# Loads of units 6 to 15 moved from GpSimd's queue to SyncE's in a fused attention and feed-forward kernel

## The chip, the cores and the metric

The kernel runs on one core of a Trainium2 chip. The metric is the device time of one execution in microseconds (us). A core has a matrix engine (TensorE, PE in the profile), three engines for elementwise work (VectorE or DVE, ScalarE or ACT, GpSimd or POOL) and SyncE (SP), which here only issues DMA transfers. Each engine works through its own instructions in order; semaphores tie the engines together. A DMA transfer can be issued by GpSimd (the profile's "software_dynamic" queue) or by SyncE ("hardware_dynamic").

## The reference

Linear attention on 8 batches and 8 heads of 576 tokens with 64 dimensions, then a feed-forward layer with an ELU.

```python
q_s = exp(q - max(q, -1)); q_s = q_s / (sum(q_s, -1) + 1e-09)
k_s = exp(k - max(k, 2));  k_s = k_s / (sum(k_s, 2) + 1e-09)     # over the tokens
kv  = einsum('bhsd,bhse->bhde', k_s, v)
x   = einsum('bhsd,bhde->bhse', q_s, kv)      # then (B, S, H*D) -> 4608 x 512
h   = x @ w_in                                # 512 -> 2048
g   = where(h > 0, h, exp(min(h, 0)) - 1)
out = g @ w_out                               # 2048 -> 512, float32
```

## The kernel before

The attention is cut into 16 units (NU): unit n is one half of the heads of batch n // 2. The feed-forward part is cut into nine blocks j of 512 tokens (NBLK).

For each unit, `load` (L321) fetches q, k and v, 576 KB each, into the tiles QR, KR and VR. QR and KR exist twice and are used by odd and even units in turn; VR is one tile for all units from 4 on. `stage1` (L359) takes the exponentials of q and k on ScalarE (L365, L368), casts v to bfloat16 into VB on GpSimd (L373), and on VectorE sums q, takes the reciprocal and scales q into QS (L381, L385, L389). From unit 6 on (BYDMA) the scaled q is transposed by a DMA that SyncE issues (`turn`, L428, QS to QT), and GpSimd widens the result into qsT (`widen`, L435). TensorE forms kv of the unit (`kv_mm`, L461); VectorE divides it into MBLK (`m`, L470, L474); TensorE multiplies it with qsT (`ao_mm`, L491) in two parts, and ScalarE copies the result into XT (`xt`, L513). The second part of unit n and the kv of unit n + 1 are one group of TensorE instructions, which signals once, at its end.

For each block, `hg` (L534) computes the hidden layer in eight groups of 256 features: matmuls on TensorE (L545), exp on ScalarE (L554, into one of two ESB tiles), then in most groups on VectorE a tensor_scalar with min and add (L571) and a maximum with the hidden values in PSUM (L573), which gives GT. A few early groups have another form (L565 on ScalarE, L567 on VectorE). `out_mm` (L577) multiplies GT with w_out (L583), `out_store` (L590) copies the result to one of three OSB tiles (L600) and has SyncE store it in two halves (L609).

The order of instructions on each engine is not that of the code. `Sched` collects all operations with an engine, an estimated duration and dependencies. A dependency is a buffer's reader or writer: a load into KR waits for the kv matmuls that read KR before, a load into QR for the scaling L389, a load into VR for the cast L373. `one_pass` (L132) simulates the engines and at each step takes the operation that can start first, and among nearly equal ones that with the lower key; `fluid` (L107) estimates when transfers land, with one queue for each issuing engine. The result is a fixed list for each engine, and `emit` (L194) writes it out with the semaphore waits ahead of each instruction. A waiting instruction therefore holds back all that follows it on its engine. An operation added under a gate (L727) can't be planned before a certain hidden group has started.

`load` takes the engine as an argument, with GpSimd as default. The loads of units 0 and 1 name SyncE; all others are on GpSimd, together with the loads of the weights, the casts L373 and the widening L435. SyncE has the transposes and the output stores. The call that the diff touches is the helper `loads` in `program` (L698), which hands out the loads of units 4 to 15; those of units 2 and 3 are written out at L655 to L659.

Of the kernel before, what the change touches and what calls it, by code (L numbers as in the profile page):

```python
# [255 lines left out]
class Gen:  # L256
# [357 lines left out]
    def program(self):  # L614
# [50 lines left out]
        def due(n):  # L665

            return when[n][1] + 4 if n in when else 3 + 4 * (n % 2)
# [30 lines left out]
        def loads(*tn):  # L698
            def go():
                for t, n in tn:  # L700
                    if n < NU:
                        self.load(n, t, due(n) - 20)
            return 0, go

        steps = [[first(2)], [wide(2), kv(2), loads(("q", 4), ("k", 4))],
# [110 lines left out]
```

## Time and profile before

| | |
|---|---|
| time, median of 3 runs (lowest to highest) | 311.72 us (311.62 to 311.88) |
| span of the profiled execution | 308.2 us |
| granted TensorE clock | 0.994 |
| TensorE, VectorE, ScalarE, GpSimd busy | 295.3, 202.9, 161.9, 71.5 us |
| GpSimd's issues of q, k and v loads (L329) | 42, about 0.72 us each |
| SyncE's issues: transposes, output stores | 10, 72 |
| DMA traffic | 49.39 MB, mean 160 GB/s |

The span is the time from the first to the last instruction in one profiled execution; it is a little shorter than the time of an unprofiled run. "Busy" counts the time in which an engine executes, and not the time in which it waits, branches or issues a hardware-queue DMA. GpSimd's issue of a DMA does count. GpSimd's waits in this execution were these, from the list of who waited for whom: 65.6 us in 12 waits of a KR load for the kv matmuls, 25.3 us of a VB cast for its v load, 25.2 us of a qsT cast for TensorE, 17.4 us of a QR load for VectorE's L389.

### The profile page before, as it was taken

To read this page: it belongs to the slowest core of one execution; us is meant where nothing else is said; L and a number is where in the kernel's file an instruction comes from. 1 tells how busy PE (TensorE), PEld (TensorE's weight loads), DVE (VectorE), ACT (ScalarE), POOL (GpSimd) and SP (SyncE) were. 2 spreads that over 40 slices of the span, in tenths; PEclk is the share of its full clock that TensorE was granted. 3 is DMA by queue.
4 is the path that set the end of the run, shared out by engine and by line. 5 is a ranking of instruction groups with operands and counts; after the bars stand their busy time and mean duration, and the time that the engine had idled before them with its cause. 6 is when DMAs were issued, how large, how long until landed. Compare 5 with 4: busy or idle time off the path is not lost.

```text
span 308.2 us, 4597 instructions
## 1 busy us (share of the span) xinstructions
PE 295.3 (96%) x1938; PEld 241.3 (78%) x1938; DVE 202.9 (66%) x244; ACT 161.9 (53%) x190; POOL 71.5 (23%) x84
## 2 busy tenths in 40 slices
PE   6889999989999979999999999999999999999994
PEld 6777778768788768888888888888888888888783
DVE  3837946798988969595959596866544445555500
ACT  4658667989657346464646463734343443333311
POOL 0790263441440436050505040301000000000000
PEclk9799999999999999999999999999999999999999
DMA  7999999797488684747383934031111221111122
GB/s 267 328 359 390 389 389 379 263 281 161 152 249 222 187 227 101 239 88 249 87 250 82 246 87 90 20 80 28 34 36 40 46 48 41 34 34 34 36 68 68
DMA packets 29589, 49.39 MB, mean 160 GB/s; under 512 B 13952, under 2 KB 13952, under 8 KB 29568
## 3 DMA queue, kind: packets, MB, share of 16 engines
q0 software_dynamic: 10336, 33.16, 35.2%
q1 hardware_dynamic: 19232, 15.93, 20.1%
q8 instruction: 15, 0.25, 0.3%
q14 instruction: 6, 0.05, 0.1%
HBM read 36.70 MB, written 9.44 MB: 150 GB/s over the span
## 4 chain that ended last, share of the span: by engine, by line
PE 87%; DVE 8%; ACT 3%; DMA 1%; issue 1%
PE PS L583 41%; PE PS L545 40%; PE PS L491 2%; PE PS L461 2%; DVE ESB L571 2%; DVE QS L389 1%; DMA QR<-in_q_dram 1%; DVE GT L573 1%; ACT ESB L554 1%; DVE ZQ L381 1%; DVE GT L567 1%; DVE MBLK L474 1%; PE PS L412 1%; ACT ESB L565 1%; PE PS L648 1%
## 5 line engine op out<-in xcount | busy, mean ns | idle before, releaser
L583 PE MATMUL PS<-W,GT 128*128 128x512 f32 x576 | 144.9, 393 | 1.6 <-DVE GT L573 1.6
L545 PE MATMUL PS<-XT,W 128*128 128x512 f32 x576 | 142.6, 392 | 2.2 <-DVE GT L573 0.8
L545 PEld LDWEIGHTS PS<-XT,W 128*128 128x128 f32 x576 | 107.3, 188 | 26.2 <-DVE GT L567 1.8
L583 PEld LDWEIGHTS PS<-W,GT 128*128 128x128 f32 x576 | 106.2, 188 | 24.1 <-DVE GT L573 2.6
L554 ACT ACTIVATE ESB<-PS 128x1024 f32<-128x1024 f32 x72 | 73.9, 1027 | 93.5 <-PE PS L545 93.3
L571 DVE TENSOR_SCALAR ESB<-ESB 128x1024 f32<-128x1024 f32 x64 | 55.2, 862 | 65.5 <-ACT ESB L554 65.2
L573 DVE TENSOR_TENSOR GT<-ESB,PS 128x1024 fp32r<-128x1024 f32 x64 | 78.1, 1221 | 2.2
L600 ACT ACTIVATE OSB<-PS 128x512 f32<-128x512 f32 x32 | 19.2, 599 | 37.0 <-PE PS L583 37.0
L381 DVE TENSOR_REDUCE ZQ<-QR 128x18 f32<-128x1152 f32 x16 | 21.6, 1349 | 6.5 <-ACT QR L365 6.2
L373 POOL CAST VB<-VR 128x1152 bf16<-128x1152 f32 x15 | 19.9, 1328 | 25.3 <-DMA VR<-in_v_dram 25.3
L329 POOL DMA_DIRECT2D KR<-in_k_dram x14 | 10.2, 726 | 65.6 <-PE PS L461 65.6
L389 DVE TENSOR_TENSOR QS<-QR,RZQ 128x1152 f16<-128x1152 f32 x16 | 21.7, 1358 | 0.6
L513 ACT ACTIVATE XT<-PS 128x640 fp32r<-128x640 f32 (+5 forms) x32 | 19.7, 619 | 3.1 <-PE PS L491 3.0
L365 ACT ACTIVATE QR<-QR 128x1152 f32<-128x1152 f32 x16 | 18.7, 1166 | 3.7 <-DMA QR<-in_q_dram 3.7
L435 POOL CAST qsT<-QT 128x1152 fp32r<-128x1152 f16 x10 | 13.7, 1370 | 29.6 <-PE PS L461 25.2
L368 ACT ACTIVATE KR<-KR 128x1152 bf16<-128x1152 f32 x16 | 18.6, 1162 | 0.8 <-DMA KR<-in_k_dram 0.8
L491 PE MATMUL PS<-qsT,MBLK 128*128 128x320 f32 (+3 forms) x64 | 14.2, 305 | 1.0 <-ACT XT L513 0.6
L491 PEld LDWEIGHTS PS<-qsT,MBLK 128*128 128x128 f32 x64 | 11.6, 189 | 4.4 <-ACT XT L513 1.0
L329 POOL DMA_DIRECT2D QR<-in_q_dram x14 | 10.3, 735 | 17.4 <-DVE QS L389 17.4
L567 DVE SCALAR_TENSOR_TENSOR GT<-PS,ESB 128x1024 fp32r<-128x1024 f32 x8 | 9.8, 1223 | 5.9 <-ACT ESB L565 5.9
L329 POOL DMA_DIRECT2D VR<-in_v_dram x14 | 10.0, 718 | 3.3 <-POOL VB L373 3.3
L648 PE MATMUL PS<-ID 128*128 128x128 f16 x92 | 8.7, 273 | 1.5 <-POOL ID L309 1.5
(28 smaller groups left out, 78.2 us busy)
## 6 DMA issues: line engine op xcount, KB each, us to landing
out_dram<-OSB SPq DMA_DIRECT2D x64, 128.0 KB, 2.4
QR<-in_q_dram POOLq DMA_DIRECT2D x14, 576.0 KB, 5.7
KR<-in_k_dram POOLq DMA_DIRECT2D x14, 576.0 KB, 5.0
VR<-in_v_dram POOLq DMA_DIRECT2D x14, 576.0 KB, 6.0
W<-in_moe_w_in_dram POOLq DMA_DIRECT2D x8, 512.0 KB, 8.1
W<-in_moe_w_out_dram POOLq DMA_DIRECT2D x4, 1024.0 KB, 17.7
QR<-in_q_dram SPq DMA_DIRECT2D x2, 576.0 KB, 4.5
KR<-in_k_dram SPq DMA_DIRECT2D x2, 576.0 KB, 6.9
```

The lines of the kernel that those rows point to most:

```text
L329: S.add(eng, ISSUE[eng], lambda e: e.dma_start(dst, src), key, W=[name], dma=f"{name}{eng}", nbytes=128 * 4608, follow=self.gpq if chain e ...
L373: S.add(eng, t, lambda e: e.tensor_copy(VB[:, hs, :, 0:D], v[:, hs, :, :]), key - 50, R=[vname], W=[f"VB{i}"])
L381: S.add("dve", t_dve(1152) + 60, lambda e: e.tensor_reduce(self.ZQ[i][:, :, :].rearrange("p h c -> p (h c)"), q[:, :, :, :].rearrange("p h ...
L389: S.add("dve", t_dve(1152) + 60, lambda e: e.tensor_tensor(qso, q[:, :, :, :], rz, ALU.mult), key - 3, R=[f"qR{i}", f"RZQ{i}"], W=[f"QS{se ...
L491: last = e.matmul(P[:, f * 512:f * 512 + n_], M[:, f, :], T[:, c0:c1, f * 64:f * 64 + 64], start=True, stop=True)
L513: S.add("act", t_act((h1 - h0) * n_, True), lambda e, dst=dst, src=src: e.activation(dst, src, AF.Copy), key, W=W, X=X)
L545: last = e.matmul(P[:, t * 512:(t + 1) * 512], self.W1[:, kc, tt * 128:(tt + 1) * 128], self.XT[:, kc, rc:rc + BLK], start=(kc == 0), stop ...
L554: S.add("act", t_act(1024, True), lambda e: e.activation(esb[:, :], P[:, :], AF.Exp), key, W=[f"E{i}"], X=banks)
L571: S.add("dve", t_dve(1024, 2) + 80, lambda e: e.tensor_scalar(esb[:, :], esb[:, :], 1.0, -1.0, ALU.min, ALU.add), key, X=[f"E{i}"])
L573: S.add("dve", t_dve(1024) + 90, lambda e: e.tensor_tensor(gt, esb[:, :], P[:, :], ALU.max), key, R=[f"E{i}"], W=gw, X=banks)
L583: last = e.matmul(dst, GT[:, jj, ts * 128:(ts + 1) * 128], self.W2[:, jj, :], start=(jj == 0), stop=(jj == 15))
L600: S.add("act", t_act(512, True), lambda e: e.activation(osb[:, :], src, AF.Copy), key, W=[f"O{i}0", f"O{i}1"], X=[f"b{bk}"])
```

## The change

The helper that issues the loads of units 4 to 15 passes an engine: GpSimd for units 4 and 5, as before, and SyncE from unit 6 on. The 30 loads of units 6 to 15 go from GpSimd's in-order list, and from its software queue, to SyncE's list and its hardware queue, in among the transposes and the output stores. It is meant to free GpSimd, whose casts stand in the same list behind loads that wait for their buffers.

```diff
@@ -699,7 +699,7 @@
             def go():
                 for t, n in tn:
                     if n < NU:
-                        self.load(n, t, due(n) - 20)
+                        self.load(n, t, due(n) - 20, "gp" if n < 6 else "sp")
             return 0, go
```

The planner, which sees other engines and other landing times, also writes a slightly different order for the rest. GpSimd's list shrinks from 77 to 45 rows (a row is a run of equal instructions): between the casts nothing is left from unit 6 on. SyncE's list has, for a typical unit, transpose, q load, two pairs of stores, v load, k load. ScalarE's list puts the exponentials of unit 8 (L365, L368) ahead of the first XT copy of unit 6; TensorE's list puts a hidden group (L545) ahead of each of the two ao parts of unit 6; VectorE's puts the reciprocal L385 of unit 8 earlier and the division L470, L474 of unit 7 one hidden group later. Up to the loads of unit 6 nothing is moved.

## The prediction, made before the changed kernel ran

> **What bounds the kernel now.** I read the page's first two parts, then the chain of waits, then the windows by stage, and then the timelines of TensorE, VectorE and GpSimd in the one stretch where TensorE stands still after the start.
>
> ```profile
> PE 295.3 (96%) x1938; PEld 241.3 (78%) x1938; DVE 202.9 (66%) x244; ACT 161.9 (53%) x190; POOL 71.5 (23%) x84
> ...
> PE   6889999989999979999999999999999999999994
> ...
> PE 87%; DVE 8%; ACT 3%; DMA 1%; issue 1%
> ```
>
> TensorE is busy 295.3 of 308.2 us and carries 87% of the chain, so a change to who issues loads can win back only idle TensorE time, 12.9 us in all. The windows say where that is:
>
> ```profile
> 0.00:40.00 40.00, 34.95 (x295) 29.08 (x295) 25.51 (x37) 25.65 (x29) 17.53 (x27) 0.96 1.10 349
> ...
> 54.00:66.00 12.00, 10.20 (x119) 7.44 (x118) 9.77 (x14) 10.58 (x12) 5.83 (x7) 1.00 0.81 250
> ...
> 100.00:110.00 10.00, 8.36 (x70) 6.66 (x67) 9.37 (x11) 3.92 (x5) 5.53 (x6) 1.00 0.68 179
> ...
> 150.00:200.00 50.00, 50.00 (x326) 41.14 (x324) 38.94 (x45) 26.60 (x32) 14.98 (x14) 1.00 0.51 133
> ...
> 289.00:308.20 19.20, 15.23 (x67) 11.99 (x65) 1.92 (x2) 3.42 (x5) 0.00 (x0) 1.00 0.30 68
> ```
>
> The second number of a row is TensorE's busy time. 5.05 us are lost before 40 us and 3.97 in the tail, which the change doesn't touch (its first moved load is at 54 us, its last before 190). From 110 to 289 us nothing is lost. In between, 1.80 us go in 54 to 66, 0.30 in 72 to 80 and 1.64 in 100 to 110. The last one is a single gap before the L583 at 109.49. Three timelines explain it (start, duration; TensorE, VectorE, GpSimd in turn):
>
> ```profile
> 109.49 2.11 PE L583 MATMUL PS<-W,GT 128*128 128x512 f32 x8 [1.64 <-DVE GT L573]
> ```
> ```profile
> 100.81 3.39 DVE L571 TENSOR_SCALAR ESB<-ESB 128x1024 f32<-128x1024 f32 x1 [0.43 <-ACT ESB L554]
> 104.24 1.22 DVE L573 TENSOR_TENSOR GT<-ESB,PS 128x1024 fp32r<-128x1024 f32 x1
> ...
> 106.21 1.36 DVE L389 TENSOR_TENSOR QS<-QR,RZQ 128x1152 f16<-128x1152 f32 x1
> 107.49 0.69 DVE L571 TENSOR_SCALAR ESB<-ESB 128x1024 f32<-128x1024 f32 x1
> 108.21 1.22 DVE L573 TENSOR_TENSOR GT<-ESB,PS 128x1024 fp32r<-128x1024 f32 x1
> ```
> ```profile
> 100.69 0.72 POOL L329 DMA_DIRECT2D KR<-in_k_dram  x1 [5.57 <-PE PS L461]
> 101.41 1.16 POOL L435 CAST qsT<-QT 128x1152 fp32r<-128x1152 f16 x1
> 102.49 1.16 POOL L373 CAST VB<-VR 128x1152 bf16<-128x1152 f32 x1
> ```
>
> VectorE's L571 normally takes 0.69 us, but here 3.39: it stands still until GpSimd's casts of qsT and VB are over (at 103.65) and ends 0.55 us later. VectorE then works without a break to 109.43, and TensorE waits for that. Both casts were stuck behind the K load of unit 10 in GpSimd's in-order queue: it idled 5.57 us until the kv matmuls (L461) had freed the K buffer, and only then did everything behind it run, in one bunch.
>
> **What the Trainium skill says.** "SBUF — State Buffer", section "Who interferes with whom", says that VectorE in a two-port mode (a tensor_scalar such as L571 can enter one) and GpSimd exclude each other for a whole instruction. This trace agrees: L571 takes 0.68 to 0.69 us alone, 1.64 when it meets one cast (119.33, 135.06), 3.39 here. "DMA: Bandwidth & Descriptors", section "SWDGE vs HWDGE vs iDMA", says that loads issued from SyncE don't use GpSimd at all; here each load issue costs GpSimd 0.72 us. Its section "Issuing engines are not separate DMA queues" says that all queues share the same 16 DMA engines; the trace agrees, as a transpose lands in 2.83 us alone (199.25) and in 5.3 to 7.5 beside loads. So I expect no gain in DMA speed.
>
> **The change part by part.** 30 load issues leave GpSimd (30 x 0.72 = 21.6 us) and join SyncE (six such issues at the start took 0.44 to 0.73 us each: 14 to 22 us). GpSimd is not a bound, so these microseconds are worth nothing; what counts is the waits that move. A lone 576 KB load lands in 4.0 us by the hardware queue (the first at the start) and 4.05 to 4.3 by the software queue (K loads at 118 to 150): equal.
>
> GpSimd keeps its 20 moved units' casts (ten VB, ten qsT), which now wait only for their own data and buffers. I replay SyncE's new order with the event times of before. Q6 54.4 (QS done at 53.7; behind the stores that end at 54.4), K6 58.0 (kv of unit 4), V6 58.7, Q7 62.7, K7 63.9, V7 65 (VB6 cast at 63.8, just behind L571's 62.47 to 63.16), transpose 6 at 71.2 as before, Q8 72.6, K8 73.5, V8 74.0 instead of 80.30, as VB7 is cast at about 70 instead of 78.85. Transpose 7 83.1, Q9 84.4, two pairs of stores, K9 88.4, V9 88.9 instead of 90.97 with room: VB8 is cast at about 80 instead of 89.52, and VB9 at about 94 instead of 102.49. Transpose 8 at 93.7 to 94.1, Q10, stores, K10 at 100.7, V10 at 101.2.
>
> So in 100 to 110 the VB9 cast is gone from the pair. The qsT8 cast needs the transpose (landed by 99.75 even at the old pace) and the last ao matmul of unit 7, which is one instruction group with kv of unit 8, over at 100.37; the semaphore took 0.32 us to GpSimd there. It runs at 100.69 to 101.84. L571 still meets that one cast, and ends at 101.84 + 0.55 = 102.4 instead of 104.2, 1.8 us earlier. Behind it as measured: L573 1.22, the two MBLK and their reciprocal 0.75, QS 1.36, L571 0.69, L573 1.22, gaps: the last ends at 107.65. TensorE comes free at 107.85 (109.49 less the gap of 1.64). The gap closes with 0.2 us to spare. V10 lands about 1.5 us behind K10 (spacing of back-to-back loads at the start: 4.73, 6.20, 7.80), that is at 106.2, when the next L571 (from 105.8) already runs, so its cast waits and not VectorE. Gain: 1.64, less 0.1 that I allow for so thin a margin.
>
> The stalls at 58 to 66 us (0.41, 0.55, 0.84) stay: VectorE is busy there without a break from 57.53 on, and no L571 in it is longer than 0.69. The 0.30 at 79.72 waits for L567 behind ScalarE's L565 and stays. The L571 at 79.62 (0.93) and 89.60 (1.63) get shorter, in time that TensorE doesn't wait for.
>
> One reordering comes with it: the planner now puts the exponentials of Q8 and K8 (L365, L368) ahead of the first XT copy of unit 6 on ScalarE, and TensorE's first hidden-layer group ahead of that unit's ao matmuls. By replay ScalarE reaches them at 83.3 and 84.4; Q8 and K8 land behind transpose 6 (77.70 at the old pace) at 79.2 and 80.7, so both are 3.7 us early. The exp of the hidden group (L554) starts at 86.1 and its GT is ready at 89.1, for a group due at 89.9. It costs nothing.
>
> SyncE's new waits: queued behind the waiting K loads are stores and the next transpose. Stores feed three OSB buffers, each reused some 22 us later (three store pairs 7.3 us apart); the longest new wait before a store is V12 and K12 behind stores, not the reverse. A transpose has from about 94 to 100.4 before its cast can start at all. Both are hidden. From 110 us on a qsT and a VB cast come in a pair at each kv, as at 182.07 in the trace before, where L571 took 1.64 and TensorE lost nothing.
>
> Sum: 311.72 - 1.64 + 0.1 = 310.2 us.
>
> **The rivals.** (a) The collision only moves: the V10 cast lands ahead of the L571 at 105.8 (in place of 106.2 it need only be 0.4 us sooner), which costs 1.15, and minus the 0.2 of margin TensorE waits 0.95; or a cast meets L571 at 79.6 to 83, where VectorE has under 1 us of room. Then the gain is 0.6 or less: 311.1 to 311.9. For it: casts now come when data land, not at a fixed place. Against it: L571 mostly gets in first by the replay. (b) Slower: SyncE becomes the place where things queue. A transpose, loads and stores share one queue; were loads behind a transpose to land 4 us later than I take (transposes reached 7.5 us), ScalarE would stand at K8 with L554 behind it, TensorE losing about 1 us there, and a similar loss in any of the nine later units adds up: 312.5 to 314. Against it: from 110 us loads are due a whole unit (15.7 us) later. (c) More gain: the stalls at 58 to 80 shrink also, by at most 0.41 + 0.55 + 0.84 + 0.30: 308.1 at the very best. V5 is cast 1.5 us earlier there, but nothing waited for that.
>
> **How the numbers follow.** The forecast with most of the gap closed has 0.62, (c) 0.06, (a) 0.18, (b) 0.14. A gain over 0.2% is 0.62 us; the forecast, (c) and none of (a) but its edge give faster 0.69, same 0.17 and slower 0.14. The range runs from 309.4 (a part of (c)) to 312.6 (the mild end of (b)).
>
> **What would show it.** Right: the L571 near 101 us at about 1.6 instead of 3.39, the VB9 cast at about 94, no TensorE gap near 108, TensorE idle about 1.6 us less in all, nothing lost from 110 to 289. Step by step: V8 issued near 74 and VB7 cast near 70. Wrong: a gap of TensorE with a release by VectorE's L573 near 108 or 85, ScalarE waiting for KR by DMA at 84, an ao matmul waiting for qsT, or ScalarE's L600 waiting for a store.

## The result, and the profile after

| | time, us (median, lowest to highest) | ratio to before, 95% interval |
|---|---|---|
| before, 4 executions | 311.8 (311.62 to 314.6) | |
| after, 4 executions | 308.53 (308.38 to 310.04) | 0.9889 (0.984 to 0.9938) |
| after, measured again: 21 executions against 74 of before | 308.54 against 310.5 | 0.9955 (0.9932 to 0.9977) |

The changed kernel is faster. The first measurement says by 1.1%, the later and much larger one by 0.45%, 1.4 us; it is before that moved, from 311.8 to 310.5, while after stayed at 308.5. The ratios leave out executions more than 1.5% above the fastest of the same kernel (8 of the 74 and 1 of the 21), the medians count all. Both profiled executions of these first measurements have a span of 308.2 us, so the spans alone tell nothing. The page of after, parts 1, 2 and 4:

```profile
PE 296.4 (96%) x1938; PEld 241.9 (78%) x1938; DVE 201.6 (65%) x244; ACT 161.9 (53%) x190; POOL 55.3 (18%) x54
...
PE   7789999989999999999999999999999999999994
...
PE 87%; DMA 4%; DVE 4%; ACT 2%; issue 1%; POOL 1%; SPq 0%
```

GpSimd lost 16.2 us of its 71.5 and VectorE's share of the chain halved, from 8% to 4%; DMA's rose from 1% to 4%, in the first 17 us. The windows by stage of after (the second number is TensorE's busy time):

```profile
0.00:40.00 40.00, 34.41 (x285) 28.18 (x286) 25.72 (x37) 24.64 (x28) 15.29 (x26) 0.96 1.08 345
...
100.00:110.00 10.00, 10.00 (x80) 8.23 (x79) 8.79 (x11) 4.79 (x7) 2.47 (x2) 1.00 0.72 236
...
150.00:200.00 50.00, 50.00 (x326) 41.15 (x325) 38.87 (x45) 26.66 (x32) 13.51 (x7) 1.00 0.51 133
```

TensorE has no idle time left in 100 to 110. It lost more than before ahead of 40 us (5.59 against 5.05 us), in a part that is the same in both programs, and began the rest later: the group of L545 that starts behind the 0.41 us gap, at 58.80 in before, starts at 60.76 here. From there to the end it takes 308.2 - 60.76 = 247.4 us against 308.2 - 58.80 = 249.4: the change is worth about 2.0 us in these two executions, and the start took them back. The timelines of VectorE and of GpSimd in after show the step that was at issue:

```profile
102.79 1.41 DVE L571 TENSOR_SCALAR ESB<-ESB 128x1024 f32<-128x1024 f32 x1 [0.43 <-ACT ESB L554]
```
```profile
97.67 1.15 POOL L373 CAST VB<-VR 128x1152 bf16<-128x1152 f32 x1 [6.05 <-DMA VR<-in_v_dram]
102.50 1.15 POOL L435 CAST qsT<-QT 128x1152 fp32r<-128x1152 f16 x1 [3.68 <-PE PS L461]
107.85 1.33 POOL L373 CAST VB<-VR 128x1152 bf16<-128x1152 f32 x1 [4.20 <-DMA VR<-in_v_dram]
```

The three casts now stand apart, none behind a load. L571 meets one of them and takes 1.41 us in place of 3.39.

### The profile page after: what moved, and what is told of

It reads as the page before. It is cut to its first block, busy times and chain, and to the rows that moved or that the text cites. A ratio compares the mean times of both kernels' runs of the same rounds, so it can differ in the third digit from the quotient of the medians.

```text
span 308.2 us, 4602 instructions
## 1 busy us (share of the span) xinstructions
PE 296.4 (96%) x1938; PEld 241.9 (78%) x1938; DVE 201.6 (65%) x244; ACT 161.9 (53%) x190; POOL 55.3 (18%) x54
## 4 chain that ended last, share of the span: by engine, by line
PE 87%; DMA 4%; DVE 4%; ACT 2%; issue 1%; POOL 1%; SPq 0%
PE PS L545 42%; PE PS L583 41%; DMA VR<-in_v_dram 2%; PE PS L491 2%; DMA W<-in_moe_w_in_dram 2%; PE PS L461 2%; DVE QS L389 1%; ACT ESB L554 1%; DVE ZQ L381 1%; DVE GT L567 1%; ACT ESB L565 1%; SPq L329 0%; DVE GT L573 0%; PE PS L412 0%; POOL VB L373 0%
## 5 line engine op out<-in xcount | busy, mean ns | idle before, releaser
L545 PE MATMUL PS<-XT,W 128*128 128x512 f32 x576 | 144.0, 394 | 2.5 <-DMA W<-in_moe_w_in_dram 1.0
L583 PE MATMUL PS<-W,GT 128*128 128x512 f32 x576 | 144.9, 393 | 0.0
L545 PEld LDWEIGHTS PS<-XT,W 128*128 128x128 f32 x576 | 108.6, 190 | 26.9 <-DVE GT L567 1.8
L583 PEld LDWEIGHTS PS<-W,GT 128*128 128x128 f32 x576 | 106.1, 188 | 22.0 <-DVE GT L573 0.5
L571 DVE TENSOR_SCALAR ESB<-ESB 128x1024 f32<-128x1024 f32 x64 | 52.0, 813 | 68.0 <-ACT ESB L554 67.6
L435 POOL CAST qsT<-QT 128x1152 fp32r<-128x1152 f16 x10 | 18.4, 1843 | 95.6 <-PE PS L461 91.7
L389 DVE TENSOR_TENSOR QS<-QR,RZQ 128x1152 f16<-128x1152 f32 x16 | 23.6, 1477 | 0.5
L365 ACT ACTIVATE QR<-QR 128x1152 f32<-128x1152 f32 x16 | 18.6, 1165 | 2.9 <-DMA QR<-in_q_dram 2.9
L368 ACT ACTIVATE KR<-KR 128x1152 bf16<-128x1152 f32 x16 | 18.6, 1161 | 1.6 <-DMA KR<-in_k_dram 1.6
L474 DVE TENSOR_TENSOR MBLK<-PS,RZK 64x128 fp32r<-64x128 f32 x32 | 9.3, 289 | 1.1
L648 PEld LDWEIGHTS PS<-ID 128*128 128x128 f16 x92 | 7.7, 126 | 1.7 <-POOL ID L309 1.5
L565 ACT ACTIVATE ESB<-ESB 128x1024 f32<-128x1024 f32 x8 | 8.5, 1061 | 0.1
```

What stands on the lines that cost most here:

```text
L365: S.add("act", t_act(1152, False), lambda e: e.activation(flat(q), flat(q), AF.Exp), key - 3, X=[f"qR{i}"])
L389: S.add("dve", t_dve(1152) + 60, lambda e: e.tensor_tensor(qso, q[:, :, :, :], rz, ALU.mult), key - 3, R=[f"qR{i}", f"RZQ{i}"], W=[f"QS{se ...
L545: last = e.matmul(P[:, t * 512:(t + 1) * 512], self.W1[:, kc, tt * 128:(tt + 1) * 128], self.XT[:, kc, rc:rc + BLK], start=(kc == 0), stop ...
L571: S.add("dve", t_dve(1024, 2) + 80, lambda e: e.tensor_scalar(esb[:, :], esb[:, :], 1.0, -1.0, ALU.min, ALU.add), key, X=[f"E{i}"])
L583: last = e.matmul(dst, GT[:, jj, ts * 128:(ts + 1) * 128], self.W2[:, jj, :], start=(jj == 0), stop=(jj == 15))
```

## The experiments

Twelve more runs followed, each with a profile; six of them are the two kernels unchanged. For each profile I give the same figure: from the start of the L545 group behind the 0.41 us gap near 60 us, up to which all but the one without fillers hold the same program, to the end of the span. It leaves out the start.

**More executions of both.** The kernels are unchanged.

> The kernel before, once more, to see how much one profiled execution differs from another. Theory A (one bunch of casts, as in the first profile): TensorE again loses 1.6 us in one gap near 108 us and little else between 66 and 289 us; the time is 311.7 us and the missing rest of the 3.2 us gain lies in the start. Theory B (the first profile was of an execution, 309.99 us, that lost less than most): TensorE loses 3 us or more between 66 and 130 us, in more than one gap behind VectorE.

> The changed kernel once more. Both theories: no TensorE gap after 82 us, time 308.4 to 308.8 us. Theory A: the first 54 us take less than in the profile of after on record (whose hidden groups were 1.96 us late at 60 us) and are as early as in the first profile of before. Theory B: the start varies by 1 to 2 us from run to run in both kernels and doesn't explain a difference of medians.

Before: 311.12 us against 310.5 of the 74 interleaved executions of the same kernel, ratio 1.0014 (0.999 to 1.0039); the profile has the same single gap of 1.64 and an L571 of 3.39, and 309.4 - 60.06 = 249.3 us. After: 308.54 us, no gap past 82 us, 306.3 - 58.70 = 247.6. So theory A is right on the gap and B wrong. On the start each was right in part: after is here as early as the first profile of before (58.70 against 58.80), as A said, and the start varies within each kernel, as B said. How much it varies shows in the executions further down.

**The order or the casts?** The planner changed the order of other engines too. x1 keeps all of the old plan and swaps only the issuing engine, x2 is the reverse, on the new plan:

```diff
+def moved(o): o.eng, o.dma = ("sp", o.dma[:-2] + "sp") if o.unit >= 6 else (o.eng, o.dma); return o
...
-            self.S.emit(self.S.order())
+            self.S.emit([self.to(o) for o in self.S.order()])
```

> The planned order of before on TensorE, ScalarE and VectorE is kept and only the 30 loads are taken out of GpSimd's list and put into SyncE's at their planned places. Theory of the casts (GpSimd's casts freed from the loads' waits bring the gain): about 308.5 to 309.3 us, no gap near 108. Rival, the order (the planner's new order of ScalarE, VectorE and TensorE around unit 8 brings it): 311 to 311.9 us.

> The new order on TensorE, ScalarE and VectorE, with the 30 loads in GpSimd's list again, so that its casts wait behind the loads. Theory of the casts: about 311 to 312 us with a long L571 (over 2.5 us) and a TensorE gap behind it. Rival, the order: 308.5 to 309 us.

x1: 309.2 us, ratio 0.9962 (0.994 to 0.9985), no gap, 307.8 - 60.26 = 247.5. That is the full gain without any of the new order. x2: 309.3 us, ratio 0.9954 (0.9934 to 0.9974), no gap either, 307.6 - 60.16 = 247.4. I had expected a gap there and missed. There was a long L571, but at another place; VectorE and GpSimd of x2:

```profile
90.25 3.29 DVE L571 TENSOR_SCALAR ESB<-ESB 128x1024 f32<-128x1024 f32 x1
```
```profile
90.05 0.70 POOL L329 DMA_DIRECT2D KR<-in_k_dram  x1 [4.85 <-PE PS L461]
90.75 1.16 POOL L373 CAST VB<-VR 128x1152 bf16<-128x1152 f32 x1
91.84 1.15 POOL L435 CAST qsT<-QT 128x1152 fp32r<-128x1152 f16 x1
```

So a stall of VectorE costs TensorE nothing some ten microseconds sooner, where VectorE has time in hand. In the place where it has none, x2 has the K load of unit 10 at 102.04 with only the qsT cast behind it, as its new order puts the VB cast of unit 9 ahead, at 97.92; L571 starts at 102.38 and takes 0.88. Moving the loads is enough (x1), and the new order, which includes their places in GpSimd's list, would have been enough too (x2).

**One load of thirty.** e5 is x1 with the K load of unit 10 left on GpSimd; e6 is before with that load alone moved; e7 leaves all on GpSimd and places it behind the two casts.

```diff
+    for o in seq: o.eng, o.dma = ("sp", o.dma[:-2] + "sp") if o.unit[0] >= 6 and o.unit != (10, "k") else (o.eng, o.dma)
```
```diff
+    for o in seq: o.eng, o.dma = ("sp", o.dma[:-2] + "sp") if o.unit == (10, "k") else (o.eng, o.dma)
```
```diff
+    k10 = next(o for o in seq if o.unit == (10, "k"))
+    seq.remove(k10)
+    seq.insert(1 + next(i for i, o in enumerate(seq) if o.unit == (9, "VB")), k10)
```

> Old plan with 29 of the 30 loads on SyncE; only the K load of unit 10 stays on GpSimd, just ahead of the qsT cast of unit 8 and a VB cast. Theory (that one issue, ahead of two casts, is what shuts VectorE out): L571 near 102 us takes 3.4 us again, TensorE has the 1.64 us gap near 110, and from the hidden group that follows the 0.41 us gap near 60 us to the end it is 249.4 us as in before. Rival (the gain comes from relieving GpSimd as a whole, or from several loads): L571 1.4 us, no gap, 247.5 us.

> The kernel before with 1 of the 30 loads, K of unit 10, on SyncE. Theory (the issue in front of the casts matters): L571 near 102 us takes about 1.4 us and runs between the two casts, no gap, 247.5 us from the hidden group near 60 us to the end. Rival 1 (two casts back to back are enough): L571 about 2.6 to 2.9 us, a gap of about 1 us, 248.5 us. Rival 2 (GpSimd's relief as a whole): 249.4 us and the gap of 1.64 stays.

> The kernel before, all 30 loads still on GpSimd's software queue, with K of unit 10 issued behind the casts of qsT of unit 8 and VB of unit 9 instead of ahead of them. Theory (place in GpSimd's list): as with that load on SyncE, no gap, 247.5 us from the hidden group near 60 us to the end. Rival (which queue carries the load matters): gap of 1.64 us, 249.4 us.

e5: 311.02 us, ratio 1.0027 (1.0005 to 1.005). With 29 loads gone the whole loss is there: 308.3 - 58.96 = 249.3 us. None of its 22 executions is under 310.02, where x1 has a median of 309.2. TensorE, VectorE and GpSimd of e5:

```profile
109.63 2.11 PE L583 MATMUL PS<-W,GT 128*128 128x512 f32 x8 [1.64 <-DVE GT L573]
```
```profile
100.97 3.38 DVE L571 TENSOR_SCALAR ESB<-ESB 128x1024 f32<-128x1024 f32 x1 [0.43 <-ACT ESB L554]
```
```profile
100.84 0.71 POOL L329 DMA_DIRECT2D KR<-in_k_dram  x1 [10.69 <-PE PS L461]
101.55 1.16 POOL L435 CAST qsT<-QT 128x1152 fp32r<-128x1152 f16 x1
102.64 1.16 POOL L373 CAST VB<-VR 128x1152 bf16<-128x1152 f32 x1
```

e6: 308.95 us, ratio 0.9968 (0.9946 to 0.999), no gap, 307.9 - 60.17 = 247.7: moving that one load brings the gain. The L571 took 0.70, not the expected 1.4, since in this execution the transpose of unit 8 had landed late (9.2 us) and the casts came only at 103.83. So this profile doesn't test rival 1, two casts back to back; x1 and e7 do. e7: 309.3 us, ratio 0.9983 (0.9959 to 1.0006), on its own unclear; its profile settles the first half. VectorE and GpSimd of e7:

```profile
100.79 1.42 DVE L571 TENSOR_SCALAR ESB<-ESB 128x1024 f32<-128x1024 f32 x1 [0.43 <-ACT ESB L554]
```
```profile
100.51 1.15 POOL L435 CAST qsT<-QT 128x1152 fp32r<-128x1152 f16 x1 [6.30 <-PE PS L461]
101.60 1.61 POOL L373 CAST VB<-VR 128x1152 bf16<-128x1152 f32 x1
103.16 0.72 POOL L329 DMA_DIRECT2D KR<-in_k_dram  x1
```

L571 took 1.42 us, between the two casts, and the gap near 110 is gone with all loads in the software queue. But a new gap stands later, and 307.2 - 58.80 is 248.4, not 247.5. TensorE, VectorE and the transposes (L428) of e7:

```profile
122.47 1.43 PE L545 MATMUL PS<-XT,W 128*128 128x512 f32 x5 [0.72 <-DVE GT L573]
```
```profile
118.23 2.32 DVE L389 TENSOR_TENSOR QS<-QR,RZQ 128x1152 f16<-128x1152 f32 x1 [2.16 <-DMA QT<-QS]
```
```profile
DMA to landing us min/median/max: 2.8/6.3/12.5
```

One transpose took 12.5 us to land beside three loads of GpSimd's queue (K10, V10, Q11); L389 may not overwrite QS before it has landed, then took 2.32 us beside a cast, and VectorE was late once more. So the place in GpSimd's list explains the old gap. Which queue carries the loads seems to matter in another way: in after the same line of the profile reads 2.8/2.9/4.7. That rests on one profile of e7.

**Executions without the gap.** The medians of before and after differ by about 2.0 us, but the ratio gives 1.4, and before has executions as fast as after (its lowest: 307.64 us). Four more profiles of before:

> The kernel before, one more profiled execution. Theory (the collision is a race of about 0.1 us between the K load's issue and L571, so not every execution has it): an execution under 309 us has no TensorE gap near 108 us and 247.5 us from the hidden group near 60 us to the end; one over 310 us has the gap and 249.4 us. Rival (the gap is there every time and only the start varies): 249.4 us every time.

> As for b3: the same kernel, another execution; over several of them, 1 in 3 without the gap by the theory, none by the rival.

> As for b3: the same kernel, another execution; over several of them, 1 in 3 without the gap by the theory, none by the rival.

> As for b3: the same kernel, another execution; over several of them, 1 in 3 without the gap by the theory, none by the rival.

b3 (314.34 us) and b5 (311.78 us) have the gap of 1.64: 312.5 - 63.08 = 249.4 and 310.0 - 60.52 = 249.5. b4 (308.64 us) has none: 306.8 - 59.35 = 247.5, the figure of after. VectorE and GpSimd of b4:

```profile
101.39 0.69 DVE L571 TENSOR_SCALAR ESB<-ESB 128x1024 f32<-128x1024 f32 x1 [0.43 <-ACT ESB L554]
```
```profile
101.27 0.96 POOL L329 DMA_DIRECT2D KR<-in_k_dram  x1 [6.22 <-PE PS L461]
102.23 1.16 POOL L435 CAST qsT<-QT 128x1152 fp32r<-128x1152 f16 x1
```

The issue starts 0.12 us ahead of L571, as in the executions with the gap (100.69 and 100.81 in the first profile, and 0.13 us in three others). So the order of the two starts doesn't decide, and what does stays open. Here VectorE got through: L571 took its 0.69, and the issue was stretched to 0.96. That the outcome changes from execution to execution was right, and so was its proportion, as far as six profiles of before can tell: 4 have the gap. b6 (313.43 us) is a third kind: the issue again took 0.96 and L571 0.69, but the transpose landed after 9.7 us, the casts came later and met L389 (2.32) and another L571 (1.64), with a gap of 0.86; 311.6 - 63.01 = 248.6.

The expectation that an execution over 310 us has the gap was too simple, because of the start: the same L545 group began anywhere from 58.80 (the first profile) to 63.08 us (b3). The windows of the first profile and then of b3 (third number from the right: granted clock):

```profile
16.00:20.00 4.00, 3.32 (x16) 2.62 (x16) 0.82 (x2) 1.31 (x3) 4.00 (x7) 1.00 1.13 344
20.00:24.00 4.00, 4.00 (x20) 3.30 (x19) 2.54 (x3) 3.17 (x4) 2.79 (x4) 1.00 1.35 391
```
```profile
16.00:20.00 4.00, 0.67 (x2) 0.60 (x3) 0.38 (x2) 0.28 (x2) 4.00 (x6) 0.65 1.12 330
20.00:24.00 4.00, 4.00 (x11) 3.13 (x10) 0.00 (x0) 0.88 (x1) 3.03 (x5) 0.50 1.33 394
```

b3's first hidden group waited 3.57 us for the weights W where the first profile waited 0.68 us for an XT copy, and TensorE then ran at a recorded clock of 0.50, with 11 instead of 20 matmuls in the window from 20 to 24 us. The first profile had its low clock at 8 to 16 us (0.79), where mostly fillers and the small matmuls of the attention ran. The clock is not the whole of it: x1 has the same three figures as the first profile (0.79, 1.00, 1.00) and started at 60.26, its first hidden group having waited 1.21 us for W.

**The start without fillers.** In the changed kernel, `order` returns the list without `fill`:

```diff
-        return self.fill(seq)
+        return seq
```

> The changed kernel without the 92 filler matmuls (L648) that keep TensorE busy in the first 15 us; they leave nothing that is used. If the dip of the granted clock in the first 20 us, which differs from execution to execution, is brought on by TensorE starting to work, it moves later and always into the hidden groups: 310 to 312 us, with a narrower spread. If it comes whatever TensorE does: as after, 308.0 to 313.6 us with the same spread of 1 to 2 us around 308.5.

310.48 us (309.57 to 312.49), ratio 1.0027 (1.0006 to 1.0048) to before: slower than after. The first 64 matmuls of hidden work, in the first profile of before and in e8:

```profile
17.22 15.06 PE L545 MATMUL PS<-XT,W 128*128 128x512 f32 x64 [0.68 <-DVE XT L516]
```
```profile
17.29 17.82 PE L545 MATMUL PS<-XT,W 128*128 128x512 f32 x64 [0.52 <-DVE XT L516]
```

They start almost together and take 2.8 us more without the fillers; with them after took 16.58 and 14.95 us in its two profiles. In e8 the window from 20 to 24 us has 12 matmuls in it at a recorded clock of 1.00, where before has 20 at 1.00 and b3 11 at 0.50. So in this stretch the recorded clock doesn't tell the rate. A low clock is recorded later, in the middle of the hidden work (0.66 in 67 to 72 us); from the 60 us mark e8 takes 310.6 - 61.68 = 248.9. So the loss did move into the hidden groups, as the first possibility said. A narrower spread is not seen: the times are in two clumps, 309.57 to 310.79 and 312.14 to 312.49. One profile doesn't prove what sets the clock. No experiment pointed to a kernel that beats after.

## Why the prediction was right or wrong

The first measurement, 308.53 us, lies below the stated range, and the step that failed is the first term of the sum. "Sum: 311.72 - 1.64 + 0.1 = 310.2 us" takes the median of three executions as the time of before. Its executions range over several microseconds, and the three lay close together (311.62 to 311.88) above the middle of the distribution, 310.5 us for 74 and 310.2 us for another 75. So the base was 1.2 to 1.5 us too high, and that is most of the miss of 1.7. Why they lay there stays open: only 30 of those 149 took 311.6 or more, so all four executions of the first measurements would do so by chance about once in 600 times. That something slowed the start in those first measurements is a rival that no run tests. A sign was in view: the profiled execution itself had taken 309.99 us. The gain was worked out from it, and with it as the base the same gain gives 308.45. That this comes so close to what was measured is partly luck: its start (58.80) was among the earliest, and the gain was put too low, two errors that offset each other. The prediction doesn't mention the 1.7 us between the two figures.

"The gap closes with 0.2 us to spare" was right: no gap near 108 in either profile of after. The second term was somewhat too small. "Gain: 1.64, less 0.1" counts only the idle time, but from the 60 us mark the profiles differ by 1.8 to 2.0 us. In the chain the L583 group behind the gap takes 2.11 us where the others take 1.83, so a restart costs 0.28 us more: 1.64 + 0.28 = 1.92. The allowance of 0.1 was not needed. In the opposite direction the gain is not paid in each execution: 4 of 6 profiles of before have the gap, one has a smaller one and one has none, (4 x 1.92 + 1.1) / 6 = 1.46 us on average by these few. Without b3 and b6, whose starts were the latest, it is 3 x 1.92 / 4 = 1.44. The 0.45% of the large measurement are 1.4 us.

"Both casts were stuck behind the K load of unit 10" was right, and sharper than I knew: e5 and e6 show that this single load carries the loss. Incomplete was the reading "it stands still until GpSimd's casts ... are over". Two casts in a row alone let VectorE in between them (1.41 in x1, 1.42 in e7, with the second cast stretched to 1.61); only when it started just behind a load's issue did it wait for all three (3.38 to 3.39, and 3.29 in x2), and not every time (0.69 in b4 and b6). An exclusion "for a whole instruction", with which the prediction says its trace agrees, covers the 1.64 beside one cast but not these two figures. Why VectorE is not let in between the casts then, no run shows.

The replay of SyncE held. Times in brackets are those of after less its later start of 1.96 us: V8 was issued at 77.00 (75.0 against the predicted 74), VB7 cast at 72.68 (70.7 against about 70), VB9 at 97.67 (95.7 against about 94; its load, issued behind K9 and stores, took 6.4 us to the cast), and L571 was 1.41 (predicted about 1.6). ScalarE came to Q8 and K8 at 85.24 and 86.30 and did not wait. No ao matmul of unit 6 or later waited for qsT, and from 110 to 289 us nothing was lost, with L571 at 1.63 or 1.64 beside each pair of casts. Three readings of the prediction were off, and nothing rested on them: one of the nine transposes beside other traffic landed in 3.5 us, not in 5.3 to 7.5; 30 issues at 0.44 us are 13 us, not 14; and 182.07 is where the cast starts, L571 starting at 182.35.

"So I expect no gain in DMA speed" was wrong for the transposes: their median landing went from 5.5 to 2.9 us. In after the loads stand behind them in the same queue instead of running beside them. The queue alone is not shown to be the reason: x1, with the same loads in that queue but in the old order, has 2.8/4.4/6.3. What the Trainium skill says in "DMA: Bandwidth & Descriptors", section "Issuing engines are not separate DMA queues", that queues share the engines, is not contradicted; my step from there to "no gain" was. In after TensorE waits for no transpose. Late transposes cost TensorE 0.72 us in e7 and, by way of the casts, 0.86 in b6.

Of the rivals, (a), a collision that only moves, is seen in x2, where it cost nothing, and in b6, an execution of before. In after it was missed by 0.37 us: L571 started at 107.48 and the VB cast of unit 10 at 107.85. (b), SyncE as the new place for queueing, cost TensorE nothing in after, x1 or e5. (c), shrinking stalls at 58 to 80, did not come: about 0.41, 0.55, 0.84 and 0.30 us stand in the profiles of before and after alike.

## What to carry to other kernels

When an engine that shares a resource idles behind a waiting transfer, look at what stands behind that transfer: the transfer's issue and the work behind it run in one bunch at the moment of release, and the bunch can stop a neighbour that has no time in hand. Find the one instruction that releases the bunch before moving thirty; here one load's place was the whole gain. And compare the profiled execution's time with the median before taking either as the base of a forecast: if they differ by more than the gain in question, more executions of the kernel before are worth more than a closer reading of its one profile.

## What the runs showed of the hardware that was not expected

- An L571 that starts 0.12 us behind a load's issue on GpSimd either takes 0.69 us, with the issue stretched from 0.72 to 0.96, or waits for the issue and for two casts behind it (3.39). Both happen with the same program, 4 times in 6 the second. In x2 one that started 0.34 us behind an issue with a single cast after it took 0.88.
- A DMA transpose that lands in 2.8 us with nothing beside it took 9.2 to 12.5 us in some executions beside loads of the software queue (e6, b6, e7), and never more than 4.7 where all the loads of those units stood in its own queue in the planner's order (both profiles of after). With the same loads in that queue but in the old order the longest was 6.3 us (x1).
- The start, up to the same matmul group, took 58.70 to 63.08 us over the thirteen profiles that share the same program up to there (those of before, of after and of the versions of one or the other, that without fillers left out), with the granted clock anywhere from 0.50 to 1.00 in 20 to 24 us. Without b3 and b6 it was 58.70 to 60.76.
- The recorded clock did not always tell the rate of the matmuls: in the window from 20 to 24 us, 12 matmuls stand at a clock of 1.00 in e8, 20 at 1.00 in the first profile of before, and 11 at 0.50 in b3.
